# Retention and a GELU layer on one core: the 128-token chunks of the retention worked as two sub-chunks of 64 tokens

## The chip, the core and the metric

One core of one Trainium2 chip runs the whole kernel. The metric is the device time of one execution in microseconds (us). The core's engines run side by side: TensorE multiplies matrices (in the profile PE, its weight loads PEld), VectorE (DVE) and ScalarE (ACT) work element by element, GpSimd (POOL) mostly issues loads, SyncE (SP) issues transposing copies and stores. They wait for each other by semaphores. Each engine works its own list of instructions strictly in the order in which the program gives them.

## What is computed

There are 8 batches, 8 heads, 576 tokens and 64 elements a head. For each batch and head:

```python
scores = (q @ k.T) / sqrt(64)
gamma  = 1 - 2 ** (-5 - head)
ret    = scores * where(rel >= 0, gamma ** rel, 0)   # rel = row - column
x      = ret @ v
```

The results of the 8 heads stand side by side as a matrix `x` of 4608 tokens by 512. Then `out = gelu(x @ w_in) @ w_out`, with 2048 columns in between and the exact GELU.

## The kernel before

**Retention in chunks.** A sequence is cut into four chunks of 128 tokens and a tail of 64. Within a chunk the scores are worked out directly. What earlier chunks add comes through a state, the 64x64 sum of k times v of each head, with the decay put into factors: `dv` scales v before it is used (`vh`, by DVE at L575 or, as eight smaller operations, by ACT at L572), and `dqT` scales the result at the end (L672). So the mask of a chunk (L558) holds only ones and zeros (`msk`). The first chunk of a sequence needs no state. It uses the plain v and a mask with the decay in it (`near`). A *unit* is a chunk of one batch. Batches go in pairs, and a *group* is the same chunk of both batches of a pair: 4 single units at the start, then 14 paired groups, and 4 tails, in each of which both batches share one unit.

**The matmuls of a paired group.** TensorE's 128x128 array can be split into tiles that work side by side: four of 64x64, or two of 128x64.
- scores (L535): 32 matmuls of 64x64 weights against 128 columns on four tiles. They fill four PSUM banks, which DVE masks in four instructions (L558).
- inner product with v (L600): 16 matmuls of 128x64 weights against 128 columns on two tiles.
- state (L619): 16 matmuls of 128x64 weights against 64 columns on two tiles. They add to a state that stays in one PSUM bank over the whole sequence. A copy to SBUF (`u_sb`, L456 on DVE or L461 on ACT) follows each time.
- cross (L653): 16 matmuls of 64x64 weights against 128 columns on four tiles, which bring in the state. Then DVE writes `xT` (L672).

The tails have the same steps with 64 columns (L525, L591, L653). A run of such steps between full-array matmuls is called a *visit* here.

**The GELU layer.** It works on 9 blocks of 512 tokens. x @ w_in is L701 (blocks 0 to 5) or, with seven products for eight, L966 (blocks 6 to 8). The product with w_out is L746 (block 0) or, with seven for eight, L885. ACT does the GELU. DVE makes sums of tiles that the seven products need.

**What sets the order.** The Python code that writes the program keeps its own clocks for the engines, queues and banks (`T`, `on`, `pe`, `free_time`). At each step it takes the work that these say is ready. An order once written is fixed: on the chip an engine that reaches an instruction too early waits there. The list `ORDER` gives the order of the loads on POOL. It also holds 89 settings for single places: `a` puts a scaling of v on ACT, `s` and `b` delay scores and inner products, `z`, `p` and `u` steer when retention or layer goes first. The scores of a group that comes by SP's transposing copies (L492) are held 2.5 us past their expected arrival, unless an `s` says otherwise (`S_LATE`).

**Instructions are fetched too.** TensorE's own instructions arrive by DMA, in blocks. The code has a model of that in `pe`: a block holds 128.9 matmuls with their weight loads (`CHUNK`), the first ends after 94.7, and one is taken as usable 8.6 us (`FETCH`) after TensorE is within 151 matmuls of it.

## Time and profile before

| | |
|---|---|
| time, median of 3 runs | 285.27 us (285.26 to 287.36) |
| profiled execution: first to last instruction | 283.7 us |
| TensorE busy | 278.0 us (98%), 3361 matmuls |
| VectorE / ScalarE / GpSimd busy | 199.7 / 158.8 / 114.0 us |
| granted TensorE clock | 0.998 of full speed |
| DMA engines | busy at 0.9 or more until about 190 us |
| instruction blocks for TensorE | 26 packets, 0.43 MB |

The profiled execution shows its span only. What lies around it is taken as the difference to the median, 1.55 us. In a row of the timeline, the first column is the start and the second the time from the first start to the last end. Consecutive rows overlap by about 0.17 us, since the end of a matmul lies well after the start of the next. So the time that a run of matmuls takes from TensorE is read from start to start.

### The profile page before, as it was taken

The numbers are of one execution on the slowest core, as the hardware profiler recorded it, in microseconds if no ns is written. First come the engines' busy times: TensorE is split into PE (matmuls) and PEld (weight loads), VectorE is DVE, ScalarE is ACT, GpSimd is POOL, SyncE is SP. The second block draws the span as 40 slices with busy tenths as digits, with TensorE's granted clock in tenths as the row PEclk, the third lists the DMA queues.
The fourth block names the chain that finished last, engine by engine and source line by source line (L and its number), as shares of the span: only waits on it lengthen the run. The fifth ranks groups of instructions, "written<-read, shape, count | busy, mean of one in ns | idle before, by whom it ended". The sixth has DMA issues, their size and how long they took to land.

```text
span 283.7 us, 8075 instructions
## 1 busy us (share of the span) xinstructions
PE 278.0 (98%) x3361; PEld 207.6 (73%) x3361; DVE 199.7 (70%) x412; ACT 158.8 (56%) x362; POOL 114.0 (40%) x143
## 2 busy tenths in 40 slices
PE   8989999999999999999999999999999999999994
PEld 3577666688874588548855778558888888888894
DVE  5753483979865595898178867889669968966822
ACT  5676724755456635693298874564565374665320
POOL 8979987993364465625468552000000000000000
PEclk9999999999999999999999999999999999999999
DMA  9999999999999999999999999910003000400133
GB/s 150 165 182 173 188 180 163 146 142 147 172 161 195 190 147 128 156 229 149 135 197 203 147 137 150 222 21 2 0 2 128 23 2 0 151 0 2 74 114 111
DMA packets 152804, 35.39 MB, mean 125 GB/s; under 512 B 141120, under 2 KB 148928, under 8 KB 152768
## 3 DMA queue, kind: packets, MB, share of 16 engines
q0 software_dynamic: 116832, 18.10, 95.3%
q1 hardware_dynamic: 34528, 16.26, 32.9%
q10 hardware_dynamic: 1408, 0.52, 0.7%
q8 instruction: 26, 0.43, 0.7%
q14 instruction: 10, 0.08, 0.1%
HBM read 36.70 MB, written 9.44 MB: 163 GB/s over the span
## 4 chain that ended last, share of the span: by engine, by line
PE 92%; POOL 3%; DMA 3%; issue 0%; DVE 0%; POOLq 0%
PE m L885 35%; PE hT L701 29%; PE f L966 13%; PE oT L746 5%; PE o_ps L600 3%; PE sc L535 3%; DMA w_in<-in_moe_w_in_dram 3%; POOL qk L318 2%; PE o_ps L653 1%; PE u_ps L619 1%; PE qk_ps L482 1%; POOL v_ld L318 1%; POOL w_in L291 1%; PE sc L525 0%; PE o_ps L591 0%
## 5 line engine op out<-in xcount | busy, mean ns | idle before, releaser
L701 PE MATMUL hT<-xT,w_in 128*128 128x512 bf16 (+3 forms) x560 | 87.4, 312 | 0.8 <-DMA w_in<-in_moe_w_in_dram 0.8
L710 ACT ACTIVATE g<-hT 128x512 bf16<-128x512 f32 (+2 forms) x106 | 57.7, 556 | 36.9 <-PE hT L701 36.1
L701 PEld LDWEIGHTS <-w_in 128*128 128x128 bf16 x560 | 48.4, 98 | 33.8 <-DMA w_in<-in_moe_w_in_dram 1.0
L885 PEld LDWEIGHTS <-gs 128*128 128x128 bf16 x656 | 62.2, 98 | 7.7
L885 PE MATMUL m<-w_sum,gs 128*128 128x256 bf16 (+1 forms) x400 | 47.7, 268 | 0.0
L318 POOL DMA_DIRECT2D v_ld<-in_v_dram x40 | 34.0, 854 | 19.3 <-DMA qk_ld<-in_k_dram 8.8
L318 POOL DMA_DIRECT2D qk_ld<-in_k_dram x36 | 30.4, 851 | 21.7 <-DMA qk_ld<-in_q_dram 19.1
L558 DVE TENSOR_TENSOR ret<-sc,msk 128x512 bf16<-128x512 f32 x48 | 30.2, 683 | 12.2 <-PE sc L535 12.2
L318 POOL DMA_DIRECT2D qk_ld<-in_q_dram x36 | 30.4, 851 | 16.9 <-DMA qkT<-qk_ld 6.5
L885 PE MATMUL m<-w_out,gs 128*128 128x256 bf16 x256 | 32.5, 273 | 0.0
L885 PE MATMUL m<-w_sum,g 128*128 128x256 bf16 x256 | 30.9, 273 | 0.0
L572 ACT ACTIVATE vh<-v_ld,dv 128x64 bf16<-128x64 bf16 x120 | 30.0, 339 | 0.0
L782 DVE TENSOR_TENSOR gs<-g 128x1024 bf16<-128x1024 bf16 x32 | 21.8, 686 | 9.0 <-ACT g L710 8.2
L885 PEld LDWEIGHTS <-g 128*128 128x128 bf16 x256 | 24.9, 98 | 3.9
L991 ACT ACTIVATE g<-f 128x512 bf16<-128x512 f32 x36 | 20.2, 590 | 8.9 <-PE f L966 7.5
L786 DVE TENSOR_TENSOR gs<-g 128x1024 bf16<-128x1024 bf16 x32 | 21.6, 684 | 0.0
L672 DVE TENSOR_TENSOR xT<-o_ps,dqT 128x512 bf16<-128x512 f32 (+1 forms) x32 | 18.4, 617 | 4.5 <-PE o_ps L653 4.4
L966 PEld LDWEIGHTS <-w_in 128*128 128x128 bf16 x192 | 18.8, 98 | 2.2
L461 ACT CAST u_sb<-u_ps 128x512 bf16<-128x512 f32 x15 | 8.7, 587 | 16.0 <-PE u_ps L619 16.0
L461 ACT COPY o<-m 128x512 f32<-128x512 f32 x14 | 8.2, 587 | 15.7 <-PE m L885 15.7
L987 ACT ACTIVATE g<-p 128x512 bf16<-128x512 f32 x12 | 7.6, 630 | 14.1 <-DVE p L985 14.1
L966 PEld LDWEIGHTS <-wi 128*128 128x128 bf16 x144 | 14.0, 98 | 1.6
(96 smaller groups left out, 337.6 us busy)
## 6 DMA issues: line engine op xcount, KB each, us to landing
out_dram<-o SPq DMA_DIRECT2D x27, 256.0 KB, 6.3
v_ld<-in_v_dram POOLq DMA_DIRECT2D x32, 128.0 KB, 9.1
qk_ld<-in_k_dram POOLq DMA_DIRECT2D x28, 128.0 KB, 10.7
qk_ld<-in_q_dram POOLq DMA_DIRECT2D x28, 128.0 KB, 8.6
w_in<-in_moe_w_in_dram POOLq DMA_DIRECT2D x8, 256.0 KB, 7.3
w_out<-in_moe_w_out_dram POOLq DMA_DIRECT2D x8, 256.0 KB, 8.0
out_dram<-o SPq DMA_DIRECT2D x14, 128.0 KB, 2.1
qk_ld<-in_q_dram POOLq DMA_DIRECT2D x8, 64.0 KB, 11.4
```

The source lines that it names most:

```text
L318: nc.gpsimd.dma_start(dst, src[2 * bp + jj, :, ci * C:ci * C + n, :].rearrange("h s d -> s h d"))
L461: nc.scalar.copy(dst, src)
L558: nc.vector.tensor_tensor(r, t, by, op=ALU.mult)
L572: nc.scalar.activation(vh[:, h, :], loaded[i][1][:, h, :], AF.Copy, scale=dv[:, h, ci:ci + 1])
L672: nc.vector.tensor_tensor(x_of(i)[:, :, n * x:n * x + n], o, dqT[:, :, ci * C:ci * C + n], op=ALU.mult)
L701: nc.tensor.matmul(hT[:, m, :], lhsT=w[:, cc, o:o + 128], rhs=x_tiles[t][:, cc, lo:hi], start=(cc == 0), stop=(cc == N_DM - 1))
L710: nc.scalar.activation(g_of(t, m0 // 2)[:, m0 % 2:m0 % 2 + n, lo:hi], hT, AF.Gelu)
L782: nc.vector.tensor_tensor(s.rearrange("p m a b -> p m (a b)"), g[:, :, 0, :], g[:, :, 1, :], op=ALU.add)
L786: nc.vector.tensor_tensor(s, g[:, :, :, LEFT], g[:, :, :, RIGHT], op=MINUS)
L885: nc.tensor.matmul(m[:, 0 if apart else ts, :], lhsT=a, rhs=w[:, c0:c1], start=p in begins and mm == 0 and ts == 0, stop=mm == N_DF // 2 - ...
L966: nc.tensor.matmul(m[:, y, :], lhsT=a[:, c], rhs=d[:, c], start=p in (P1, P7) and y == 0 and c == 0, stop=c == 1, skip_group_check=True)
L991: nc.scalar.activation(g[:, :, rows, cols], m, AF.Gelu)
```

## The change

Within a chunk, only the scores of each 64-token half with itself are computed. What the first half adds to the second goes through the state, which is now handed on every 64 tokens.
- scores: 32 matmuls against 64 columns, two PSUM banks, two masks.
- inner product (`inner_pair`): 32 matmuls against 64 columns on four tiles, in two passes of 16. In each pass the two row halves write to different banks; the second pass changes them over. Between the passes stands an instruction on ACT that does nothing but wait for the first pass; the second pass waits for it.
- state (`state_halves`): 16 matmuls a half. Half 1 of one batch pair and half 0 of the other go together on four tiles where both are ready, else one half alone on two tiles. Each half is followed by a copy to SBUF.
- cross: up to 32 matmuls against 64 columns, the two halves with their own state.
- The four batch pairs go in two twos: chunk by chunk in turn, pairs 0 and 1, then 2 and 3. So two states stay in PSUM, one for each pair. Pairs 2 and 3 no longer use `near` for their first chunk but `msk` and `dqT`, for which POOL makes one more piece of `dqT`.
- All settings for single places are gone from `ORDER`, and `FETCH` is 7.0.

```diff
@@ units and groups
-    for bp in range(B // 2):
-        for ci in range(0 if bp > 1 else 1, NCI - 1):
-            groups.append([len(units), len(units) + 1])
-            units += [(bp, ci, 0), (bp, ci, 1)]
-        groups.append([len(units)])
-        units.append((bp, NCI - 1, None))
+    for two in ((0, 1), (2, 3)):
+        for ci in range(1 - two[0] // 2, NCI - 1):
+            for bp in two:
+                groups.append([len(units), len(units) + 1])
+                units += [(bp, ci, 0), (bp, ci, 1)]
+        for bp in two:
+            groups.append([len(units)])
+            units.append((bp, NCI - 1, None))
...
-             "wo2 wo3 q7 wo4 k7 dq3 q11 b4+1.0 wo6 v8 wo5 q6 k8 wo7 v6 v7 k9 q10 q9 a28 k11 q8 v11 k10 q12 dq4 v9 "
-             "v10 a5 k12 v12 b19+6.0 a24 a27 a26 s4+1.5 z32+3 z8+5 b11+1.5 a23 z23+2.2 s2+0.6 p32+28 p31+28 z18+5 "
...
+             "wo2 wo3 q7 wo4 k7 dq3 dq4 dq0 wo6 v6 wo5 q6 wo7 v7").split()
...
-    FETCH, FETCH_IDLE = 8.6, 2.5
+    FETCH, FETCH_IDLE = 7.0, 2.5
...
+    def state_halves(todo):
...
+        for h in range(H):
+            for j in range(2):
+                for n, x in todo:
+                    bp, ci, _ = units[groups[n][0]]
+                    i, sl = groups[n][j], slice(L * x, L * x + L)
+                    nc.tensor.matmul(u_bank[bp][1][64 * j:64 * j + 64, h, :], lhsT=loaded[i][0][sl, 1, h, j, :], rhs=st[i]["vh"][sl, h, :],
+                                     start=(ci == 0 and x == 0 and h == 0), stop=(h == H - 1), skip_group_check=True)
...
@@ scores
-        got = [[bank([128, HP, 128], FP32, "sc") for _ in range(2)] for _ in g]
+        got = [bank([128, H, L], FP32, "sc") for _ in g]
         for h in range(H):
-            for c in range(2):
-                cols = slice(64 * c, 64 * c + 64)
+            for x in range(2):
+                cols = slice(L * x, L * x + L)
                 for j in range(2):
                     sl = slice(64 * j, 64 * j + 64)
-                    nc.tensor.matmul(got[j][h % 2][1][cols, h // 2, :], lhsT=qkT[sl, 1, h, cols], rhs=qkT[sl, 0, h, :],
-                                     start=(h < 2), stop=True, skip_group_check=True)
+                    nc.tensor.matmul(got[j][1][cols, h, :], lhsT=qkT[sl, 1, h, cols], rhs=qkT[sl, 0, h, cols],
+                                     start=(h == 0), stop=True, skip_group_check=True)
...
+    def inner_pair(n, swapped):
...
+        for hp in range(HP):
+            for e in range(2):
+                for x in range(2):
+                    i, sl = g[1 - x if swapped else x], slice(L * x, L * x + L)
+                    nc.tensor.matmul(st[i]["o"][0][1][64 * e:64 * e + 64, hp, sl], lhsT=st[i]["vh"][sl, 2 * hp + e, :],
+                                           rhs=st[i]["ret"][0][sl, 2 * hp + e, :], start=(swapped and hp == 0), stop=False,
+                                           skip_group_check=True)
+        if swapped:
+            nc.scalar.clobber_nop([nc.scalar.lower_ap(st[i]["o"][0][1]) for i in g])
...
@@ cross
+        parts = [0] if j0 is None else [x for x in range(2) if ci or x]
+        for x in parts:
+            u, cols = u_tile[bp, ci, x], slice(L * x, L * x + L)
+            for hp in range(HP):
+                for e in range(2):
+                    for j in range(2):
+                        o = st[g[0]]["o"][j][1] if j0 is None else st[g[j]]["o"][0][1]
+                        sl = slice(64 * j, 64 * j + 64)
+                        nc.tensor.matmul(o[64 * e:64 * e + 64, hp, cols], lhsT=u[sl, 2 * hp + e, :], rhs=qT[sl, 0, 2 * hp + e, cols],
+                                         start=False, stop=(hp == HP - 1 and x == parts[-1]), skip_group_check=True)
```

## The prediction

> **What bounds the kernel now.** I read the page's table of busy time first, then TensorE's waits, then the timeline of single visits, and last the queues.

> ```profile
> PE 278.0 (98%) x3361; PEld 207.6 (73%) x3361; DVE 199.7 (70%) x412; ACT 158.8 (56%) x362; POOL 114.0 (40%) x143
> ...
> PE hT L701 <- DMA w_in<-in_moe_w_in_dram: 0.8, 1, 0.8
> ...
> q8 instruction: 26, 0.43, 0.7%
> ```

> TensorE is busy 98%, and after its first matmul its waits hold one entry, 0.8 us. So the time is the sum of TensorE's work, and each us taken from it counts until something else makes it wait. The whole profiled time is 283.7 us of span plus 1.55 us around it.

> The price of each matmul is read in the timeline, from start to start:

> ```profile
> 80.29 0.64 PE L600 MATMUL o_ps<-ret,vh 128*64 128x128 bf16 x16
> 80.76 0.42 PE L619 MATMUL u_ps<-vh,qk_ld 128*64 128x64 bf16 x16
> 81.11 0.42 PE L653 MATMUL o_ps<-qkT,u_sb 64*64 64x128 bf16 x16
> 81.35 0.62 PE L535 MATMUL sc<-qkT 64*64 64x128 bf16 x32
> 81.90 0.94 PE L885 MATMUL m<-w_sum,gs 128*128 128x256 bf16 x7
> ...
> 110.41 0.32 PE L591 MATMUL o_ps<-ret,vh 64*64 64x64 bf16 x16
> 110.56 0.62 PE L535 MATMUL sc<-qkT 64*64 64x128 bf16 x32
> 111.01 0.29 PE L653 MATMUL o_ps<-qkT,u_sb 64*64 64x64 bf16 x16
> ```

> At 110.56, 32 score matmuls take 0.45 us: 14.06 ns each, since four tiles share a round of 56 ns. At 80.29, 16 inner products take 0.47: 28.1 ns each, two to a round, and 0.02 of handing over. The state is 15.8 ns a matmul, two to a round of 31.6 ns with 64 columns. On four tiles with 64 columns, 16 matmuls take 0.15 us (110.41): the same 31.6 ns a round, so 7.9 ns each, and 0.02 of handing over. Changing between the full array and tiles costs 0.104 us each way, between two and four tiles 0.10 (81.90 less 81.35 is 0.55 for 0.45 of scores). With these prices all of TensorE's list before sums to 277.4 us to its last start; the trace has 278.6. The rest is the 0.8 us wait and 0.3 us of small ones.

> **The change on TensorE, from the order of the two programs.**
> - Scores: 448 matmuls at 14.06 ns become 448 at 7.9: 6.30 to 3.54 us.
> - Inner products: 256 at 28.1 ns (7.19 us) become 448 at 7.9 and, for the four single units, 32 at 28.1: 4.44 us.
> - State: 256 at 15.8 ns (4.04 us) become 32 at 15.8 and 448 in 18 runs of 16 or 32. Ten runs pair two halves, eight go alone on two tiles, and each takes 0.253 us: 5.06 in all, 1.0 more.
> - Cross: 192 at 14.06 and 64 at 7.9 (3.21 us) become 480 at 7.9: 3.79, 0.6 more.
> - Changes of mode and handing over: 8.7 to 8.0 us. Four warming matmuls fewer at the start: 0.87 us less. Smaller pieces of L701: 0.1 more.

> Together 277.4 becomes 272.0: **5.4 us less**. All of it is on the path, as nothing else ended a wait.

> **Beside TensorE.** DVE loses 20 masks (13.7 us at 683 ns) and 8 with `near` (5.5). It gains the 15 scalings that the settings had put on ACT (10.5 at 700 ns), four results of first chunks instead of one (2.0), 12 copies of the state (8.3) and two small ones: 2.6 us more, 202 of 280. ACT loses those scalings (30.0 us of 120 operations) and gains about nothing. The new piece of `dqT` on POOL (1.06 us, as the two of its size at L299) delays the loads queued behind it by no more than that. Loads, transposing copies and stores are the same in number. None of this is on the path as long as TensorE has other work that is ready, and when the last paired scores start, at 190.3 us, 93 us of TensorE's work still follow, nearly all of it the layer's. So I cost it at nothing. If that cover is missing, it is the third rival.

> **What it adds: blocks of instructions that come late.** A paired visit now has 128 matmuls in about 1.3 us, 3361 become 4061, and an instruction block holds 129. Summing my prices between the borders that the code gives: before, TensorE never takes less than 7.1 us for a block (7.1 at 62 to 69 us). After the change it is 3.6, 4.6, 3.0, 4.0 and 4.1 us for five of them, around 49, 64, 132, 136 and 178 us. The trace has the packets of the instruction queue. While the DMA engines are loaded, one landed 3.8 to 6.8 us, in the mean 5.6, after TensorE was 161 matmuls short of needing it (the lead that gives the least scatter, 0.8), with 4.2 us or more to spare. After the change TensorE covers that lead in 5.2, 5.6 and 5.8 us at the closest places. Letting each block be late by what is missing, and each delay help the next block: 0.4 us in all at 5.6, 3.8 us at 6.8, 13.6 us at 8.6 (as if a block could be used 3 us after it landed; the spare 4.2 us before excludes no more than that), 0 at 5.2. I take 1.5, by the mean with its scatter and a little for starting again.

> [...]

> **What it adds: a wait by way of ACT.** In each of 14 visits the second pass of inner products waits for an instruction on ACT that itself waits for the first pass. Between them lie the state (0.27 us) and in 11 visits scores too (0.27 more). A 64-column matmul ends about 0.2 us after its start, and two semaphore hops follow. No row shows the detour. Its ends: 0, and 14 x 0.6 = 8 us if each time a GELU (596 ns) stands in front on ACT. I take 1.0, 0.2 to 0.3 in the three visits with one short cover and little elsewhere: the row nearest is TensorE's wait list, which has no waits for ACT. Queued behind the waiting pass are the cross and all of the layer's next matmuls; queued behind the ACT instruction are GELUs, which had to wait for TensorE anyway.

> **The sum:** 283.7 - 5.4 + 1.5 + 1.0 = 280.8 us of span, and with 1.55 around it **282.4 us**. What a measurement of this kernel can tell from no change is about 1%, 2.9 us, so this stands at the border of faster and same.

> **The rivals.**
> 1. *Blocks never late*, and the detour costs next to nothing: 285.3 - 5.4 + 0.5 = 280.4. For it: 4.2 us to spare before. Against: the lead is covered in half the time. Chance 0.24.
> 2. *Slower: blocks are usable only well after they land.* Place: the visits around 49, 76, 132 to 136, 166 and 180 us, where two visits follow within some 40 matmuls. With 1.0 for the detour, it eats the gain from 4.4 us of lateness on, that is from a delivery of 7.0 us within that lead. At 7.6 us it costs 6.9 (287.8), at 8.6 us 13.6 (294.5). For it: the code itself reckons with 7.0 us from a lead of 151, which in my sum gives 6.3 us. Against: the trace's landings, 5.6. Chance 0.24, middle 289.
> 3. *The order without its 89 settings fits the chip less well.* Retention's loads keep the DMA engines at 0.9 or more up to 190 us, and the new order asks for them sooner: the twelfth full group's scores stand at 144 us of TensorE's sum, where before they stood at 157, with its copies landed at about 150. Settings that held scores back 2.5 us are still the default, so about 3 us of 5 are left. With smaller waits of DVE, which has 59 us of work in 70 between 115 and 184 us, I give it 5: 287. Chance 0.14.
> 4. *Four tiles don't keep up the round of 31.6 ns* through 100 matmuls; the rows show it over 16 only. At the 14.06 ns of the long score run, 1824 matmuls would cost 11 us more. Half of that, with the forecast's other terms: 288. Chance 0.10.

> **How the numbers follow.** The forecast's own case has 0.28 and runs from 281.4 to 283.9, half of it on each side of the border at 282.4. Faster by over 1%: rival 1 and half the forecast, 0.38, with 0.02 from rival 3 where its price is nothing: 0.40. Within 1%, 282.4 to 288.1: the other half, and what of rivals 2 to 4 lies below 288: 0.29. Slower by over 1%: 0.31, most of it rival 2. Cases of both signs hold much of the chance. The range reaches down to 279.3, below rival 1 without any price (279.9) by what my sum may be off, and up to 292, which leaves out the dear end of rivals 2 and 4.

> **What would show it.** Scores at 0.25 us for 32 matmuls and inner passes at 0.15, or else rival 4. TensorE gaps that end with no semaphore ("issue", or no releaser at all) a little after an instruction packet lands, in visits about 49, 76, 136 and 166 us: the block term, and its size. Waits of the second pass for ACT's sequencer: the detour. Waits of scores for transposing copies, or of the layer for DVE: rival 3. An instruction queue of about 32 packets, DVE near 202 us and ACT near 128 would show that the change does what it says. I am wrong if TensorE's busy time doesn't fall, or if it falls and idle time of over 5 us stands in its place.

## The result, and the profile after

The changed kernel is **slower**: 297.13 us in the median (296.23 to 299.08) against 286.31 us of the kernel before beside it, a ratio of 1.041 with a 95% interval of 1.036 to 1.046. The forecast was 282.4 us with a range of 279.3 to 292.0. One of the four runs of before (289.94 us) counts as slow and is left out of the ratio; without it their median is 285.27 us.

The profiled execution is the longest of the four: 299.08 us, of which 297.3 are its span. The page of the changed kernel, table of busy time, granted clock in 40 slices, and the queue of TensorE's instructions:

```profile
PE 277.8 (93%) x4044; PEld 208.9 (70%) x4061; DVE 203.2 (68%) x416; ACT 132.1 (44%) x242; POOL 114.9 (39%) x144
...
PEclk9999999999999999999979998999999999999999
...
q8 instruction: 32, 0.52, 0.8%
```

TensorE's busy time has not fallen (277.8 against 278.0), its share has (93% against 98%), and in two slices the granted clock is below full. Busy time is no measure of the list here: it also counts what the lower clock adds, and the 0.2 us by which a matmul's record reaches into the gap behind it. TensorE's waits (us in total, times, longest):

```profile
PE sc L594 <- issue: 4.7, 2, 2.7
PE u_ps L493 <- issue: 2.3, 1, 2.3
PE m L969 <- issue: 1.9, 1, 1.9
PE warm L1276 <- DVE zeros L124: 1.2, 1, 1.2
PE o_ps L738 <- issue: 1.1, 2, 0.8
```

"Issue" is idle time that no semaphore ended. Only the 1.2 us for `zeros` is old. No long wait for data, for VectorE or for ScalarE has come. The timeline shows the longest of these standstills, in the middle of a visit:

```profile
145.01 0.32 PE L683 MATMUL o_ps<-ret,vh 64*64 64x64 bf16 x16
145.16 0.43 PE L493 MATMUL u_ps<-vh,qk_ld 64*64 64x64 bf16 x32
145.41 0.46 PE L594 MATMUL sc<-qkT 64*64 64x64 bf16 x31
148.60 0.19 PE L594 MATMUL sc<-qkT 64*64 64x64 bf16 x1 [2.72 <-issue]
148.60 0.32 PE L683 MATMUL o_ps<-ret,vh 64*64 64x64 bf16 x16
148.75 0.43 PE L738 MATMUL o_ps<-qkT,u 64*64 64x64 bf16 x32
149.11 3.92 PE L969 MATMUL m<-w_sum,gs 128*128 128x256 bf16 x20
```

TensorE stops before the last score matmul. In the trace an instruction packet landed at 147.1 us, 1.5 us before TensorE goes on. The prices hold: the inner passes take 0.15 us, the state 0.25, the cross 0.36 with its change of mode. But the 20 matmuls of the layer at 149.11 take 3.71 us to the next start, where 20 cost 2.2. The view by windows, with the granted clock in the column before the last two:

```profile
138.00:145.70 7.70, 7.48 (x241) 6.41 (x240) 5.59 (x12) 2.37 (x5) 4.04 (x5) 1.00 2.32 136
145.70:148.60 2.90, 0.18 (x22) 0.10 (x9) 1.29 (x2) 0.56 (x1) 2.09 (x3) 1.00 3.64 74
149.70:153.10 3.40, 3.40 (x18) 2.28 (x16) 3.25 (x7) 0.00 (x0) 1.90 (x3) 0.50 3.21 134
```

After the standstill the clock is 0.50 for 3.41 us. This happens once more, at 183.8 us.

**The account.** I laid the actual start of each matmul beside the sum of the prediction's prices over the same list. Where the difference jumps, TensorE lost time. Before, it is 2.4 us at the end, all of it from the first 30 us. After, it is 19.4.

| from before to after, spans 283.7 to 297.3 | us |
|---|---|
| TensorE's list, 277.4 to 272.0 | -5.4 |
| eight standstills at borders of instruction blocks (1.02, 2.07, 0.40, 2.15, 0.30, 0.41, 2.90, 2.48) | +11.7 |
| two stretches at half clock | +3.6 |
| small waits, a third of them in the first 30 us | +1.7 |
| from the last matmul's start to the end, 3.9 to 5.9 | +2.0 |
| sum | +13.6 |

All eight standstills lie on one grid: after 93.3 matmuls and then every 127.75. With as many weight loads that is 255.5 instructions, and each of the 32 packets of the queue has 16 KB. In six of the eight TensorE goes on 1.4 to 1.7 us after its block's packet has landed, in the one at 124 us 2.0 and in the one at 117 us 3.0 us after. Why these two took longer is open. In changed_tail below, with the same list, the block of the one at 117 us took 1.5.

The last row is in the view of SyncE's and VectorE's last instructions, first of the kernel before, then of the changed one:

```profile
278.03 2.67 SPq L729 DMA_DIRECT2D out_dram<-o  x4
...
280.04 0.29 DVE L846 TENSOR_TENSOR o<-m,o 128x128 f32<-128x128 f32 x1 [0.15 <-PE m L885]
```

```profile
289.89 4.38 SPq L813 DMA_DIRECT2D out_dram<-o  x6
...
291.62 0.29 DVE L930 TENSOR_TENSOR o<-m,o 128x128 f32<-128x128 f32 x1 [0.16 <-PE m L969]
```

Before, SyncE's last store is issued as VectorE ends (280.36 against 280.33). After, it is issued at 293.88, 2.0 us after VectorE has ended: with batch pairs in twos, the last block of 512 tokens ends in two tails, each stored in two pieces, and SyncE's row of stores grows.

### The profile page after: what moved, and what is told of

It is laid out like the page before. It is cut to its first block, busy times and chain, and to the rows that moved or that the text cites. A ratio compares the mean times of both kernels' runs of the same rounds, so it can differ in the third digit from the quotient of the medians.

```text
span 297.3 us, 9360 instructions
## 1 busy us (share of the span) xinstructions
PE 277.8 (93%) x4044; PEld 208.9 (70%) x4061; DVE 203.2 (68%) x416; ACT 132.1 (44%) x242; POOL 114.9 (39%) x144
## 3 DMA queue, kind: packets, MB, share of 16 engines
q0 software_dynamic: 116832, 18.10, 95.8%
## 4 chain that ended last, share of the span: by engine, by line
PE 88%; issue 4%; POOL 4%; DMA 2%; DVE 0%; POOLq 0%
PE m L969 34%; PE hT L785 27%; PE f L1050 12%; PE oT L830 5%; DMA qk<-in_q_dram 2%; PE o_ps L683 2%; PE sc L594 2%; PE u_ps L493 2%; PE o_ps L738 2%; POOL qk L328 1%; PE qk_ps L541 1%; POOL w_in L300 1%; POOL v_ld L328 1%; PE o_ps L657 0%; PE sc L584 0%
## 5 line engine op out<-in xcount | busy, mean ns | idle before, releaser
L794 ACT ACTIVATE g<-hT 128x512 bf16<-128x512 f32 (+2 forms) x107 | 58.9, 553 | 55.4 <-PE hT L785 54.5
L785 PEld LDWEIGHTS <-w_in 128*128 128x128 bf16 x592 | 50.5, 98 | 32.2 <-issue 0.6
L969 PEld LDWEIGHTS <-gs 128*128 128x128 bf16 x656 | 63.6, 100 | 10.8 <-issue 2.1
L969 PE MATMUL m<-w_sum,gs 128*128 128x256 bf16 (+1 forms) x400 | 50.8, 279 | 0.0
L328 POOL DMA_DIRECT2D qk_ld<-in_q_dram x36 | 30.3, 848 | 22.4 <-DMA v_ld<-in_v_dram 12.2
L641 DVE TENSOR_TENSOR vh<-v_ld,dv 128x512 bf16<-128x512 bf16 x36 | 24.5, 702 | 2.0 <-DMA v_ld<-in_v_dram 1.9
L758 DVE TENSOR_TENSOR xT<-o_ps,dqT 128x512 bf16<-128x512 f32 (+1 forms) x36 | 20.9, 623 | 3.6 <-PE o_ps L738 3.5
L609 DVE TENSOR_TENSOR ret<-sc,msk 128x512 bf16<-128x512 f32 x28 | 18.7, 681 | 4.1 <-PE sc L594 4.1
L1050 PEld LDWEIGHTS <-w_in 128*128 128x128 bf16 x192 | 18.7, 98 | 2.5 <-DVE xs L1023 0.3
L515 DVE CAST u<-u_ps 128x512 bf16<-128x512 f32 x13 | 9.0, 689 | 12.1 <-PE u_ps L493 10.8
L520 ACT CAST u<-u_ps 128x512 bf16<-128x512 f32 x17 | 10.0, 586 | 16.4 <-PE u_ps L493 14.6
L830 PE MATMUL oT<-w_out,g 128*128 128x512 bf16 x58 | 14.8, 380 | 0.5 <-issue 0.3
## 6 DMA issues: line engine op xcount, KB each, us to landing
qk_ld<-in_q_dram POOLq DMA_DIRECT2D x28, 128.0 KB, 10.3
qk_ld<-in_q_dram POOLq DMA_DIRECT2D x8, 64.0 KB, 10.2
```

Of the source, the lines that this page charges most:

```text
L328: nc.gpsimd.dma_start(dst, src[2 * bp + jj, :, ci * C:ci * C + n, :].rearrange("h s d -> s h d"))
L609: nc.vector.tensor_tensor(r, t, msk.to_broadcast([128, H, L]), op=ALU.mult)
L641: nc.vector.tensor_tensor(vh, loaded[i][1], dv[:, :, ci:ci + 1].to_broadcast([128, H, D]), op=ALU.mult)
L758: nc.vector.tensor_tensor(x_of(i)[:, :, n * x:n * x + n], o, dqT[:, :, ci * C:ci * C + n], op=ALU.mult)
L785: nc.tensor.matmul(hT[:, m, :], lhsT=w[:, cc, o:o + 128], rhs=x_tiles[t][:, cc, lo:hi], start=(cc == 0), stop=(cc == N_DM - 1))
L794: nc.scalar.activation(g_of(t, m0 // 2)[:, m0 % 2:m0 % 2 + n, lo:hi], hT, AF.Gelu)
```

## The experiments

The first theory: blocks of instructions come late because retention's matmuls, with the same work, are too many in too short a time while the DMA engines are loaded. A theory of this kind can be tested from both sides, by making blocks scarce in the kernel before, and plentiful in the changed one.

**cut.** The kernel before with its order untouched. Score and cross matmuls of paired groups are cut in two of 64 columns: 640 matmuls more, no work more.

```diff
-                    nc.tensor.matmul(got[j][h % 2][1][cols, h // 2, :], lhsT=qkT[sl, 1, h, cols], rhs=qkT[sl, 0, h, :],
-                                     start=(h < 2), stop=True, skip_group_check=True)
+            for y in range(2):
+                ys = slice(64 * y, 64 * y + 64)
...
+                        nc.tensor.matmul(got[j][h % 2][1][cols, h // 2, ys], lhsT=qkT[sl, 1, h, cols], rhs=qkT[sl, 0, h, ys],
+                                         start=(h < 2 and y == 0), stop=True, skip_group_check=True)
```

> The kernel before, its order untouched, with each score and cross matmul of the paired groups cut into two of 64 columns: the same results, 640 matmuls more, and 128 to a visit, as in the changed kernel. Theory (instruction blocks are late): the prices of the rows add 1.1 us; with blocks usable 7.8 us after TensorE comes within 150 matmuls of them, five or six visits (about 38, 83, 101, 115, 163, 188 us) stand still for 6 us together (2.3 at 7.2 us, 10.3 at 8.4): 292, between 288.5 and 297. Rival (the gaps come from what is new in the structure: the two passes with the detour by ACT, the copies of the state): 285.3 + 1.1 = 286.4, no gaps.

Measured: 297.62 us (297.31 to 299.33), ratio 1.043 (1.038 to 1.048): as slow as the changed kernel, without any part of its new order, and 0.6 us above the theory's range. Five standstills at borders took 8.6 us, where 6 were expected, and the clock was at half once, for 3.41 us from 171.07 on, which the theory had left out. TensorE's waits, and the longest standstill in the timeline:

```profile
PE sc L537 <- issue: 7.4, 4, 4.3
PE warm L1191 <- DVE zeros L118: 1.2, 1, 1.2
PE o_ps L602 <- issue: 0.4, 1, 0.4
```

```profile
166.60 0.54 PE L537 MATMUL sc<-qkT 64*64 64x64 bf16 x43
171.46 0.48 PE L537 MATMUL sc<-qkT 64*64 64x64 bf16 x21 [4.31 <-issue]
```

TensorE stops between two score matmuls. The packet landed at 169.98, and 1.5 us later it goes on.

**half_loads.** The changed kernel's TensorE list word for word, but a third of the bytes of its busiest queue gone (11.80 MB for 18.10). The second batch of each pair is left out from the 5th unit on: its q, k and v are written as zeros by GpSimd, not loaded.

```diff
-            nc.gpsimd.dma_start(dst, src[2 * bp + jj, :, ci * C:ci * C + n, :].rearrange("h s d -> s h d"))
+            if i >= 4 and jj == 1:
+                nc.gpsimd.memset(dst, 0.0)
+            else:
+                nc.gpsimd.dma_start(dst, src[2 * bp + jj, :, ci * C:ci * C + n, :].rearrange("h s d -> s h d"))
```

> The changed kernel with TensorE's list the same, word for word; from the fifth unit on, the second batch of each pair isn't loaded (its q, k and v are zeros that GpSimd writes), so about half of the loads' packets are gone. It leaves out the results of those batches. Theory (blocks are late because the DMA engines are full): blocks land sooner, gaps shrink from 11.7 us to 1 or 2, the clock doesn't drop: 297.1 - 11.7 - 3.6 + 1.5 = 283. Rival (a block takes its time whatever the load, or TensorE's list alone makes the gaps): 297.

Measured: 285.31 us (283.34 to 286.87), ratio 0.999 (0.996 to 1.001). TensorE's waits:

```profile
PE hT L788 <- DMA w_in<-in_moe_w_in_dram: 1.7, 1, 1.7
PE warm L1279 <- DVE zeros L124: 1.2, 1, 1.2
PE u_ps L705 <- DVE vh L644: 0.9, 1, 0.9
PE oT L833 <- issue: 0.3, 2, 0.2
PE warm L1272 <- issue: 0.2, 1, 0.2
```

No standstill at a block's border is left. So the same instructions in the same order lose 12 us at the borders or nothing, by whether these loads are made. But 285.3 is not 283, and that had to be explained too.

**half_loads_before** and **cut_half_loads.** The same edit in the kernel before and in *cut*, for the other two corners.

> The kernel before, its order untouched, with the same half of the loads left out as in half_loads: the q, k and v of the second batch of each pair, from the 5th unit on, are written as zeros by GpSimd (so those batches of the output are left out). Theory (the change's gain on TensorE is real, and half_loads gave it away by its own edit): half_loads lost 2.9 us at its start, in waits of 1.7 for w_in and 1.1 for the state, and 1.8 in small waits after that, which its edit brings. Then this kernel loses the same 2 to 4 us and takes 287.5 to 289.5, so that with blocks in time the changed order is 2.5 to 4 us ahead. Rival (the gain of 5.4 us is not there, whatever the blocks do): 284 to 286, as half_loads.

> The kernel of cut (640 matmuls more, no work more, order untouched, 297.6 us) with half of the loads left out as in half_loads. Theory (cut lost its 12 us because blocks of instructions came late behind the loads): with the blocks in time it stands within 1.5 us of the kernel before with the same loads left out, 285 to 290, and TensorE has no idle time ended by an instruction packet of over 0.5 us. Rival (640 more matmuls with their weight loads cost TensorE time by themselves, about 19 ns each): 295 or more.

Measured: 285.74 us (285.38 to 286.51) and 287.62 us (287.47 to 288.17). *cut* loses 12.2 us under full loads and 1.9 with these loads left out. In cut_half_loads no standstill at a border is left. So 640 matmuls cost 3 ns each by themselves, and 10.3 us by their late blocks: 8.6 of standstills, 1.7 of the halved clock. For the changed kernel the theory of half_loads_before missed: the edit costs the kernel before nothing, so what the changed order lost beside its blocks was its own.

**late_half_changed** and **late_half_before.** The zeros begin with the 9th unit, after the first 30 us.

```diff
-            if i >= 4 and jj == 1:
+            if i >= 8 and jj == 1:
```

> The changed kernel's order word for word, with the second batch's q, k and v of a pair written as zeros from the 9th unit on, not from the 5th (those parts of the output are left out), so that the first 30 us, in which half_loads lost 2.9 us to waits for w_in and for the state, are as in the changed kernel. Theory (the 5.4 us that the rows give for TensorE are real, and half_loads hid them behind its own early waits): 272.0 of TensorE's sum with the 2.4 of lag that the kernel before has too, 1 to 2 us of small waits, and what lies around: 281 to 283.5, and 2.5 to 4.5 us below late_half_before. Rival (with blocks in time the changed order loses the rest by other small waits): 284.5 to 286, level with late_half_before.

> The kernel before, its order untouched, with the same loads left out as in late_half_changed. Both theories: 285 to 286, as the kernel before, since nothing waited for a block or a load there.

Measured: 285.24 us (284.42 to 286.92) and 285.90 us (285.60 to 286.55). The theory missed once more. The account of late_half_changed: -5.4 for the list; four late blocks 2.1; 2.6 of small waits more than before; and 1.4 more from the last matmul to the end (5.5 against 4.1). The last of these terms had not been tested: SyncE's row of stores.

**late_half_tail** and **changed_tail.** Two of these stores go by GpSimd, which is idle then (busy 0.00 us from 188 us on in the changed kernel). TensorE's list stays as it is, in late_half_changed and in the changed kernel.

```diff
-                store(t, 2 + x, hi[:, x, LEFT], 0, 256)
+                store(t, 2 + x, hi[:, x, LEFT], 0, 256, *[nc.gpsimd if x else nc.sync] * 2)
```

> late_half_changed (285.24 us) with one thing more: in the last block of 512 tokens the two stores of the left half of the fourth unit go by GpSimd instead of SyncE. In the changed kernel the last block ends in two tails, each stored in two pieces, and SyncE issues its last store 2.0 us after VectorE has written it (293.88 against 291.91), in the kernel before at once (280.36 against 280.33); from the start of the last matmul to the end it takes 5.9 us (5.5 in late_half_changed) against 3.9. TensorE's list is the same word for word. Theory (SyncE's row of stores sets the end): from the last matmul's start to the end 4.0 to 4.4 us, and 283.8 to 284.4 in all. Rival (the end is set by something else, a landing of the last store or the waits at the close): 5.3 to 5.6, 285.2.

> The changed kernel with the same two stores on GpSimd, nothing left out. Theory: from the last matmul's start to the end 4.0 to 4.4 us instead of 5.9, so 295.4 where the changed kernel took 297.1, within its scatter of 2 us by late blocks. Rival: 5.9 us as before, 297.1.

Measured: 283.30 us (282.95 to 283.50), ratio 0.990 (0.988 to 0.992), and 295.07 us (291.56 to 297.33), ratio 1.028 (1.022 to 1.034). From the last matmul's start to the end it took 4.2 and 3.8 us. TensorE's waits in late_half_tail:

```profile
PE warm L1279 <- DVE zeros L124: 1.2, 1, 1.2
PE qk_ps L544 <- DMA qk<-in_q_dram: 0.7, 1, 0.7
```

No block is late in this execution. Its account closes: 285.9 of late_half_before, -5.4 for the list, +2.8 of small waits, +0.2 at the end, 283.5; measured 283.3. That is a little below the theory's 283.8 to 284.4. The stores account for 1.2 us of the 1.9 to late_half_changed (5.5 to 4.2 at the end). That no block is late is most of the rest; the stores do not explain it, and no run shows what does. The forecast's gain on TensorE is there when the blocks are. In changed_tail the late blocks stayed (the profiled execution, the fastest of the four, has standstills of 1.06, 2.34, 1.05 and 2.63 us among others, 7.9 in all). The two stores were worth about 2 us by the end (5.9 to 3.8); the median, 2.1 us lower, shows that less well, as the four runs spread over 5.8 us.

**no_settings.** The kernel before without the 89 settings of `ORDER`, for the third rival.

> The kernel before without its 89 settings for single places. Theory (the settings are not what the change lost): by the rows its list is 0.9 us shorter, and 1.3 us of one late block come in: 285.7, within 1% of before. Rival (the settings fit the order to the chip, and the change lost that): 290 or more.

Measured: 287.29 us (286.98 to 288.24), ratio 1.006 (1.005 to 1.008): within the 1% of the theory, though 1.6 us above its 285.7. The settings are worth 1.9 us in the order that they were made for.

**spaced** and **spaced_less.** Can the changed order be laid so that no block is late? The code's model of blocks gets the borders and the lead of the trace, and a visit is put off when it, or the 40 matmuls behind it, would meet a block that isn't there. *spaced* reckons with 8.5 us from the lead to use, *spaced_less* with 7.8.

```diff
-    CHUNK, FIRST_CHUNK, ASKED = 128.9, 94.7, 151.0
-    FETCH, FETCH_IDLE = 7.0, 2.5
+    CHUNK, FIRST_CHUNK, ASKED = 127.75, 93.3, 150.0
+    FETCH, FETCH_IDLE = 8.5, 3.55
...
+                if fn == "S" and ready <= now:
+                    n = 96 * bool(a[1]) + 32 * bool(a[0])
+                    late = late_by(n, 0.25 + ROUND * n / 4)
+                    if late > 0.25:
+                        acts[x] = now + min(late, 0.5), fn, a
```

> The changed kernel with an order that puts a visit off while, by the trace's numbers (a block every 127.75 matmuls from 93.3 on, usable 8.5 us after TensorE is within 150 of it), it or the 40 matmuls behind it would wait for a block. The work is the same. Theory (blocks are late, and nothing else is): TensorE's sum is 272.3 by the rows, lateness 0.4 to 3, no drop of the clock: 282, between 280 and 284.5. Rival (the gaps hide waits for data of the new structure, which come out when the blocks are on time): 287 or more.

> As spaced, but the planner puts a visit off by a delivery time of 7.8 us instead of 8.5, so retention ends 5.5 us earlier on TensorE's list (at 211.5 us of its sum, against 217 in spaced and 208.5 in the changed kernel). Spaced lost 5.5 us to late blocks and 1.6 to the halved clock by 93 us, nothing from 93 to 205 us, and 6.2 us to waits of the layer for VectorE at 210 to 235 us, after its late retention. Theory (delivery is about 7 us with its scatter, 9 at most, so both losses shrink): 0.6 to 4 us of late blocks, 2 to 3 of waits at the end, 282 to 288. Rival (delivery behind the loads is no figure that an order can be planned by: whatever visits are put off, others meet a landing of 9 to 10 us): 291 or more.

Measured: 297.31 us (295.07 to 300.70) and 298.12 us (295.16 to 299.15). Both missed. The view of *spaced* by windows, with TensorE's busy time in the third column:

```profile
60.00:95.00 35.00, 29.95 (x580) 23.48 (x580) 19.58 (x34) 12.15 (x21) 15.16 (x20) 0.95 1.81 175
95.00:205.00 110.00, 109.53 (x1513) 75.23 (x1521) 75.73 (x153) 49.89 (x85) 44.96 (x54) 1.00 1.66 133
205.00:236.00 31.00, 26.02 (x606) 21.28 (x606) 29.62 (x54) 12.95 (x24) 0.00 (x0) 1.00 0.18 45
```

From 95 to 205 us nothing is lost any more. But from 60 to 95 us TensorE lacks 5 us: blocks took up to 10.2 us from the lead to landing there, where 7 had been allowed for. And from 205 to 236 us it lacks 5 more, with VectorE busy 29.6 of 31: retention ends later, and the layer has to wait for its sums (1.7 us for `p`, 1.0 each for `m` and `f`). *spaced_less* has five late blocks of 0.2 to 1.5 us from 61 to 91 us, and the waits at the end as well. The time is that of the rival of *spaced_less* (291 or more). That delivery under load is no figure to plan an order by is what these two orders suggest; others were not tried.

**stands.** The clock by itself. The kernel before, with nine standstills put into its last 90 us, in each of which TensorE waits by a semaphore for GpSimd.

```diff
+        nc.tensor.matmul(t, lhsT=held_up[:, :128], rhs=zeros, start=True, stop=True)
+        for lo in range(0, w, 500):
+            nc.gpsimd.memset(held_up[:, :max(128, min(500, w - lo))], 0.0)
+        nc.tensor.matmul(t, lhsT=held_up[:, :128], rhs=zeros, start=True, stop=True)
```

> The kernel before, with nine standstills of TensorE put into its last 78 us, where only full-array matmuls of the layer are left: each time TensorE waits by a semaphore for GpSimd, which fills a piece of a tile; by the 0.55 to 0.6 us of a fill of 512 columns the idle times are about 1.8, 2.0, 2.2, 2.45, 2.65, 3.1, 2.1, 2.3 and 2.55 us, some 6.5 us apart. No work is left out. Theory (the granted clock halves for 3.4 us after any standstill of 2.3 us or more, whatever caused it): stretches at 0.5 after the 4th, 5th, 6th and 9th, perhaps after the 8th, none after the first two; 285.4 + 21 of standing + 4 of the added matmuls + 1.9 for each halving = 318 to 321. Rival (the halving belongs to late instruction blocks alone, or needs more than 3.1 us): no stretch at 0.5, 309 to 312.

Measured: 316.12 us (315.24 to 317.01), below the theory's 318 to 321: 20.4 of standing, 3.9 of added matmuls, 5.9 for four halvings, 1.5 each instead of 1.9. The number of halvings is as expected, but not which: a standstill of 2.32 us was followed by one, and the two longest, 2.83 and 3.14, were not. The rival falls too, since these standstills wait for no block. What tells them apart is the place. The halvings begin at 246.97, 257.20, 298.17 and 308.40 us, all whole multiples of 3.413 us apart, and 3.413 us is how long each half-speed stretch of the changed kernel lasts in its trace. With windows of that length laid on these marks, the windows around the 3rd and the 6th standstill:

```profile
243.55:246.96 3.41, 1.25 (x10) 0.70 (x8) 1.23 (x3) 0.47 (x1) 1.81 (x4) 1.00 0.00 0
246.97:250.38 3.41, 3.41 (x18) 2.41 (x16) 2.12 (x5) 1.12 (x2) 0.00 (x0) 0.50 0.01 2
274.28:277.69 3.41, 1.63 (x14) 1.11 (x12) 1.51 (x3) 1.62 (x3) 1.54 (x3) 1.00 0.00 0
277.69:281.10 3.41, 2.21 (x20) 1.90 (x21) 0.72 (x2) 0.59 (x1) 1.03 (x2) 1.00 0.00 0
281.10:284.51 3.41, 3.41 (x34) 3.06 (x32) 3.31 (x7) 1.25 (x3) 0.00 (x0) 1.00 0.00 0
```

The 2.32 us lie in one window, and the next has 0.50. The 3.14 us lie across a mark, 1.95 and 1.19, and the clock stays at 1.00. The same marks, reckoned from each execution's first full clock, sort the standstills of the other runs. Idle is counted here from a matmul's start plus its columns at 2.4 per ns to the next start, a rate of my choice, a little above the traces' (512 columns take 216 ns from start to start, 2.37 per ns, and 256 take 109, 2.35), in gaps of over 0.3 us, and summed over each window:

| idle in one window, us | clock in the next |
|---|---|
| 1.84, 1.95, 2.05 (stands), 2.07 (changed kernel, the standstill of 2.07 at 81 us), 1.90 (changed_tail, a standstill of 2.61 across a mark) | 1.0 |
| 2.10 (spaced), 2.20, 2.32, 2.35, 2.41 (stands), 2.31, 2.47 (changed kernel), 2.34 (changed_tail), 2.58 (spaced_less), 3.41 (cut) | 0.5 |

The line between the two rows is no sharper than the count: with gaps down to 0.05 us taken in, its nearest values are 2.07 and 2.20.

**No version beats the kernel before.** The best of the changed order with all its work done is changed_tail. The 283.3 us of late_half_tail leave out part of the loads and of the output.

## Why the prediction was wrong, by its steps

- **TensorE's list, -5.4 us: right.** An undisturbed visit of 128 matmuls takes 1.28 us from its first start to the layer's next, within 0.1 us of its prices, and late_half_tail shows the gain once nothing hides it. The sign that was named against it, TensorE's busy time not falling, did come (277.8 against 278.0), but by the clock and the gaps, not by the list. The fourth rival falls: four tiles keep the round of 31.6 ns through 128 matmuls.
- **Beside TensorE: right about the engines.** VectorE 203.2 us (forecast 202), ScalarE 132.1 (128), 32 instruction packets, no long wait for data. Costed at nothing, though, and not nothing, were small waits: 1.7 us here and 2.8 in late_half_tail.
- **The detour by way of ACT, 1.0 us: too dear.** No second pass waits for ScalarE in the list of waits, and in late_half_tail only two of them, at 86 and 179 us, start 0.1 us later than by the prices. What the prediction did not have: three crosses there, at 87, 149 and 180 us, take 0.2 to 0.3 us more than their price. Why is open.
- **Late blocks, 1.5 us: the step that failed.** They took 11.7. The mechanism was that of the second rival, and so were most of the places. These were given along TensorE's sum, and the trace runs behind that by what it has lost so far, 17 us in the end: the blocks around 49, 76, 132, 136 and 166 us are those of the standstills at 53, 81, 141, 149 and 183 us (8.9 us together). The one at 180 was in time, and those at 107, 117 and 124 us (2.9) were not foreseen. But I sized the forecast by landings of 5.6 us after a lead of 161 matmuls. Four things were off in that term. A landed block could be used only 1.3 to 1.7 us later, in nearly all late blocks of all runs. I knew that nothing excluded up to 3 us, and still put 0 into the sum. The lead is nearer 150 than 161: after the loads are over, the changed kernel's landings scatter by 0.5 us around a lead of 150 and by 0.6 around 160. The borders lie 127.75 matmuls apart, not 128.9, which shifts the 20th by 24. And the landings of the kernel before were taken over unchanged, where in the changed kernel they rose to 7.4 us in the mean from 100 to 190 us, and to 10.3 at most, from 77 to 87 us (5.9 and 10.5 in changed_tail, with the same list). With 150 and 7.8 us from lead to use, a value taken after the result, my replay of the list gives 10.2 us.
- **The clock: not foreseen.** It was read as 0.998 in the kernel before, in which TensorE waits 1.2 us at the longest, and taken to stay there. It cost 3.6 us that the prediction put at nothing.
- **The end, 3.9 us after the last matmul: taken over unchanged, and wrong by 2.0 us.** I counted that the number of stores stays (48 before, 49 after) and did not ask where in SyncE's order they come.
- **The sum.** The profiled execution took 299.1 us, 16.7 more than forecast: 10.2 for late blocks (11.7 less the 1.5), 3.6 for the clock, 2.0 for the end and 1.7 for small waits, less 1.0 for the detour, make 16.5.
- **The rivals.** The first falls: 11.7 us of standstills at borders speak against it. The third was of a plausible size but hidden: 1.9 us for the settings in the old order, 2.8 of small waits in late_half_tail; whether settings would save those was not tried. The second's dear end, 294.5, left out the clock and the end of the kernel; with both it would have given 300.

## What to carry to other kernels

Count instructions as well as time: where a faster form needs more matmuls, look up how long TensorE takes for one instruction block in the densest place, and hold that against lead, landing under the load of that stage (here a lead of 150 matmuls and then 7.4 us in the mean, from 100 to 190 us), and the 1.3 to 1.7 us that nearly all late blocks here took from landing to use. Under these loads a kernel with 4 us to spare lost 12 once 640 matmuls were added. And when units change places, go through the last few instructions of each queue again: what followed TensorE's last matmul here was on the path with its whole length, 3.9 us before and 5.9 after.
